# Top-k attention with a low-rank mixer and an MLP: where in a pair's fourth step the call stands that moves on a slab of parameters

## The chip, the cores and the metric

The kernel runs on one core of one Trainium2 chip, as one launch. The metric is the time of the whole launch on the device, in microseconds; the median of four runs before the change is 1765.66 us (1764.82 to 1766.17). The engines are named as the profile names them: PE is TensorE (matmuls; PEld its weight loads), DVE is VectorE, ACT is ScalarE, POOL is GpSimd, SP is SyncE, which here only issues DMAs. Each engine works through its own list of instructions in order and waits on semaphores for the others.

## What is computed

There are 8 batches, 8 heads, 576 positions and 64 values for each head. The first block is attention in which each row keeps only its 32 largest scores; its output, with the heads side by side (512 channels), goes into a low-rank mixer over the positions and an MLP over the channels (512 to 2048 to 512). The mixer's and the MLP's parameters come as 64-bit floats, q, k and v as 32-bit floats.

```
scores = (q @ k^T) / sqrt(64)
kth    = 32nd largest of each row
attn   = softmax(where(scores >= kth, scores, -1e9)) @ v
x      = attn with heads side by side               # (8, 576, 512)
u      = x + ((x^T @ U) @ V)^T                      # U: 576x32, V: 32x576
out    = u + max(u @ w_ch1, 0) @ w_ch2              # 512x2048, 2048x512
```

## The kernel before

**Steps.** The heads are taken in pairs, 4 pairs for each batch, 32 pairs in all. A pair has 5 steps: t = 0 to 3 take 128 rows of both heads (two score tiles of 128x576, called chunk 0 and chunk 1), and t = 4 takes the last 64 rows of both heads in one tile. Steps are numbered n = 5g + t through all pairs. One loop over n writes the instructions of all engines in an order set out by hand; no scheduler reorders them. The loop has three forms: one for the first batch's steps (n below 19, `ALONE` is 20), one for the two steps in which the first batch is finished (n = 19 and 20), and one for all later steps. In the later steps the MLP of the batch before is laid between the attention's work; in the first batch there is none yet.

**A step's selection.** For a score tile, VectorE finds the 8 largest values of each row (L385), and then in three rounds replaces those found by a very small number (L396) and finds the next 8 (L400). The last value of the third round is the 32nd largest. The generator `front` holds this: its first `next` gives L385, the next three the rounds 1 to 3. Behind round 3 the scores below the 32nd are pushed down. For chunk 1 GpSimd does it: a mask (L403) and an addition (L404). For chunk 0 it is done early in the following step: ScalarE makes the offset (L420) and the mask (L421), and GpSimd subtracts (L422). Then ScalarE takes the exponentials of both chunks (L351), in the middle of the following step. Three buffers for score tiles go round, so a new tile of scores is copied from PSUM (L344 to L346, on ScalarE) only where the exponentials of three steps before are done. In step 18 chunk 0 goes another way: ScalarE takes the exponential early, and VectorE multiplies it by the mask (L406) right behind round 3.

**Behind the exponentials.** TensorE transposes the weights (L475, L480), ScalarE copies them (L476, L481), TensorE multiplies with v (L509, L513, L499) and ScalarE copies the result (L522, L507). When a pair is through, `mixed` transposes back (L534, L538), divides by the sums on GpSimd (L539), and applies U and V (L545, L553, L557, L559, L567). After a batch's fourth pair the MLP's first products (L582, with ScalarE's L594) and second products (L601) follow.

**Parameters.** The 64-bit parameters come in 36 slabs, most of them 128x512 values. Each is turned to 32-bit floats by integer work on its words, in a line of three stages, and `next_params(1)` moves that line on by one slab. In this order a call

- issues what is left of the passes of the slab begun in the call before, on ScalarE: L174, L175, L178,
- joins that slab: a shift by 3 bits on VectorE (L186) and two integer additions on GpSimd (L187, L189),
- makes the slab loaded in the call before ready for its three passes; they are then issued one by one by the following calls of `fill` (or by the next call of `next_params`),
- issues the load of another slab on SP (L152).

So a slab is loaded in one call, passed over ScalarE after the next, and joined in the one after that. Three buffers hold the raw slabs. In the first batch's steps a call stands behind round 1 where t is 0 to 3, and a second one behind round 3 where t is 0 or 1; t = 4 has none. That makes 6 calls for a pair.

**fill.** Each `fill()` issues one waiting pass on ScalarE, moves `mixed` on by one stage, and, once there is an MLP to do, issues a share of it.

A step of the first batch is written in this order: what is left of chunk 0 of the step before (L420 to L422), the scores of the next step (on TensorE and ScalarE), the products with v of three steps before, transposes of two steps before, `fill`, round 1, a call of `next_params`, `fill`, round 2, the exponentials of the step before, `fill`, round 3, for t of 0 and 1 a second call, the mask and the addition for chunk 1 (L403, L404), `fill`.

Of the kernel before, what the change touches and what calls it, by code (L numbers as in the profile page):

```python
# [26 lines left out]
def kernel(  # L27
# [35 lines left out]
    NT, TAIL = 4, 64  # L63
# [221 lines left out]
    def prep(g):  # L285

        qkT = attn.tile([P, 2, S], F32, tag="qkT", name="qkT")
        qkTs[g] = qkT
        if blocked(g):
            nc.vector.transpose(qkT.rearrange("p i n -> p (i n)"), raw.pop(g))  # L290
            yield
            return
        tiles, ends = raw.pop(g)
        for i in (0, 2, 1) if g == 0 else (0, 1, 2):
            if i == 2:
                tp = ps_t.tile([P, 2, TAIL], F32, tag="tp", name="tp")
                nc.tensor.transpose(
                    tp.rearrange("p i n -> p (i n)"), ends.rearrange("p h d -> p (h d)"), ident
                )
                nc.scalar.copy(qkT[:, :, MAIN:S], tp)  # L300
                yield
                continue
            tp = ps_t.tile([P, NT, P], F32, tag="tp", name="tp")
            for c in range(NT):
                nc.tensor.transpose(tp[:, c, :], tiles[i][:, c].rearrange("p h d -> p (h d)"), ident)
            copy = nc.vector.tensor_copy if g == 0 and i else nc.scalar.copy
            copy(qkT[:, i, 0:MAIN], tp.rearrange("p t n -> p (t n)"))
            yield
# [54 lines left out]
    def eased(g, t):  # L363
        return bool(ways(g, t)[2])
# [70 lines left out]
    def shared(g, t):  # L435


        return t < NT and g * CH + t >= ROUNDED
# [22 lines left out]
    def turns(g, t):  # L461


        E2 = probs.pop((g, t))
        nh = 2 if t < NT else 1
        if shared(g, t):
            PT = PTs[g, t]
        else:
            PT = attn.tile([P, 2 * NT + 1, P], F32, tag="PT", name="PT")
            PTs[g, t] = PT  # L470
        for h in range(1 if shared(g, t) else nh):
            tp = ps_t.tile([P, NT, P], F32, tag="tp", name="tp")
            for j in range(NT):
                a = h * (S + TAIL) + j * P
                nc.tensor.transpose(tp[:, j, :], E2[:, a : a + P], ident)  # L475
            nc.scalar.copy(PT[:, NT * h : NT * h + NT], tp)  # L476
            yield
        tp = ps_t.tile([P, P], F32, tag="tp", name="tp")
        a = MAIN if nh == 2 else S - P
        nc.tensor.transpose(tp, E2[:, a : a + P], ident)  # L480
        nc.scalar.copy(PT[:, NT * nh], tp)  # L481
        yield

    def inverse(g, lo, hi):
        den = dens[g][:, lo:hi]
        if g == NPAIR - 1:
            nc.vector.tensor_scalar_add(den, den, 1e-9)
        nc.vector.reciprocal(den, den)

    def values(g, t):  # L490

        PT = PTs.pop((g, t))
        va, vd, vt = (a[g % NV] for a in (vas, vds, vts))
        O = ps_t.tile([P, P], F32, tag="tp", name="O")
        if t == NT:
            den, x = dens[g], xs[g % 2]
            inverse(g, 2 * NT if g == NPAIR - 1 else 0, 2 * NT + 1)
            for j in range(NT + 1):
                nc.tensor.matmul(  # L499
                    O,  # L500
                    lhsT=PT[:, j],
                    rhs=va[:, :, j, :] if j < NT else vt,
                    start=(j == 0),
                    stop=(j == NT),
                )
            for h in range(2):
                nc.scalar.mul(x[half(h), NT, half(h)], O[half(h), half(h)], den[half(h), 2 * NT :])  # L507
            return
        nc.tensor.matmul(O, lhsT=vd, rhs=PT[:, 2 * NT], start=True, stop=False)  # L509
        PB = PT[:, NT : 2 * NT].rearrange("p a (c j) -> p c a j", c=NT) if shared(g, t) else None  # L510
        for j in range(NT):
            for h in range(2):
                nc.tensor.matmul(  # L513
                    O[half(h)],
                    lhsT=va[:, h, j, :],
                    rhs=PB[:, j] if h and shared(g, t) else PT[:, NT * h + j],
                    start=False,
                    stop=(j == NT - 1),
                )
        if t == 0:  # L520
            XTs[g] = attn.tile([P, MAIN], F32, tag="XT", name="XT")
        nc.scalar.copy(XTs[g][:, cols(t)], O)  # L522
# [173 lines left out]
    t = 0  # L696
# [5 lines left out]
    for n in range(STEPS + 2):  # L702
        g, t = divmod(n, CH)
        if n < STEPS:
            if t == 0 and g + 1 < NP:
                load(g + 1)
            if t == 1 and g + 1 < NP:
                ready = prep(g + 1)
            fronts[n] = front(g, t)
            next(fronts[n])  # L710
        here, last = fronts.get(n, iter(())), fronts.pop(n - 1, iter(()))
        if n >= ALONE - 1 and n <= ALONE:

            if n < ALONE:
                next(last)
                values(*divmod(n - 3, CH))
                list(turning)
                next(here)
                next(last)
                scores(*divmod(n + 1, CH))  # L720
                values(*divmod(n - 2, CH))
            list(turns(*divmod(n - 1, CH)))
            values(*divmod(n - 1, CH))
            if n < ALONE:
                next(here)
                next(here)
                inverse(g, 0, 2 * NT)
                mixing.append(mixed(g, 1))
                fill()
                next(here)  # L730
                continue
            fill()
            scores(*divmod(n + 1, CH))
            next(here)
            while mixing:
                fill()
            next_params(1)
            fill()
            next(last, None)
            next(here)  # L740
            fill()
            next(here)
            next(here)
            fill()
            continue
        ease = eased(*divmod(n - 1, CH))
        if n < ALONE:
            if ease:
                next(last, None)
            scores(*divmod(n + 1, CH))  # L750
            if n >= 3:
                values(*divmod(n - 3, CH))
                if (n - 3) % CH == NT:
                    mixing.append(mixed((n - 3) // CH, 3))
            list(turning)
            fill()
            next(here)
            if t < NT:
                next_params(1)
            fill()  # L760
            next(ready, None)
            next(here)
            next(last, None)
            fill()
            next(here)
            if t in (0, 1):
                next_params(1)
            next(here)
            fill()
            if n >= 1:  # L770
                turning = turns(*divmod(n - 1, CH))
            continue
        away = n <= STEPS and shared(*divmod(n - 1, CH))
        if ease:
            next(last, None)
        fill()
        next(turning, None)
        fill()
        next(turning, None)
        if away:  # L780
            next(last)
        fill()
        next(turning, None)
        fill()
        if ease:
            next(last, None)
        if n - 2 >= ALONE:
            values(*divmod(n - 2, CH))
        if n + 1 < STEPS:
            scores(*divmod(n + 1, CH))  # L790
        next(here, None)
        next_params(1)
        if n - 2 >= ALONE and (n - 2) % CH == NT:
            mixing.append(mixed((n - 2) // CH, 5))
        fill()
        next(here, None)
        if away:
            blocks(*divmod(n - 1, CH))
        fill()
        if n <= STEPS:  # L800
            turning = turns(*divmod(n - 1, CH))
        fill()
        next(here, None)
        next(ready, None)
        if t in (1, 3):
            next_params(1)
        next(here, None)
        fill()
# [33 lines left out]
```

## Time and profile before

| what | value |
|---|---|
| median of 4 runs | 1765.66 us |
| profiled execution, its own time | 1766.04 us |
| its span, first to last instruction | 1764.3 us |
| PE busy | 1659.9 us (94%) |
| VectorE busy | 1540.1 us (87%) |
| ScalarE busy | 1027.4 us (58%) |
| GpSimd busy | 847.3 us (48%) |
| mean granted TensorE clock | 0.976 |
| DMA, mean | 64 GB/s |

The page cuts the span into 40 slices of 44 us; each digit is the busy share of an engine in tenths. Steps 0 to 18 of the first batch run from about 11 to 196 us, and the first product of an MLP starts at 212 us. The shares over the whole span are averages over these two stages. The timeline shows each instruction with its start, its duration, its line and operation, and in brackets how long the engine had been idle before and for whom. An instruction can be shown to start some 0.08 us before the one ahead of it on its engine ends. The chain of waits follows back from the last instruction, at each step to what released it.

### The profile page before, as it was taken

What the parts mean: (1) busy time and instruction counts of PE and PEld (TensorE: products, weight loads), DVE (VectorE), ACT (ScalarE), POOL (GpSimd) and SP (SyncE); (2) the same over time, 40 slices, a digit from 0 to 9 for tenths busy, and PEclk for the clock granted to TensorE, in tenths of its full rate; (3) what the DMA queues carried; (4) which work ended last, traced back from release to release, by engine and by line L of the source; (5) the groups of instructions that cost most, each with busy time, mean ns of one, the idle gap of its engine ahead of it and who ended that gap; (6) DMA issues with size and microseconds to landing.
All of it is one profiled execution on the core that took longest, in us unless ns stands there. A gap on an engine that the chain in (4) does not pass through costs nothing.

```text
span 1764.3 us, 28973 instructions
## 1 busy us (share of the span) xinstructions
PE 1659.9 (94%) x9851; PEld 1251.4 (71%) x9851; DVE 1540.1 (87%) x3106; ACT 1027.4 (58%) x2682; POOL 847.3 (48%) x591
## 2 busy tenths in 40 slices
PE   4565789999999999999999999999999999999999
PEld 2443556777777877788777877788777877788677
DVE  7999989999999999999999999999999999994000
ACT  4778777665655656565655566565656656564100
POOL 4777677444545454444444454545354554543000
PEclk7788899999999999999999999999999999999999
DMA  3232222233222222332322222323222232311010
GB/s 92 84 90 78 76 78 60 50 72 72 67 67 66 66 67 63 72 70 67 70 64 68 63 68 63 75 66 73 63 63 73 59 75 58 77 44 46 4 15 12
DMA packets 275828, 112.78 MB, mean 64 GB/s; under 512 B 173920, under 2 KB 260192, under 8 KB 275680
## 3 DMA queue, kind: packets, MB, share of 16 engines
q1 hardware_dynamic: 274624, 110.68, 26.0%
q8 instruction: 77, 1.26, 0.3%
q14 instruction: 71, 0.58, 0.1%
q10 hardware_dynamic: 1056, 0.26, 0.1%
HBM read 74.15 MB, written 36.70 MB: 63 GB/s over the span
## 4 chain that ended last, share of the span: by engine, by line
PE 77%; DVE 13%; POOL 4%; ACT 3%; issue 1%; DMA 1%; SPq 0%; POOLq 0%; DVEq 0%
PE mm L582 26%; PE mm L601 25%; PE sc L333 6%; PE O L513 6%; DVE rr L396 6%; DVE m L400 5%; PE tp L475 3%; DVE first L385 2%; PE sc L320 2%; PE O L499 2%; PE up L557 1%; PE O L509 1%; POOL E L403 1%; PE up L559 1%; PE tp L649 1%
## 5 line engine op out<-in xcount | busy, mean ns | idle before, releaser
L400 DVE MAX8 m<-rr 128x8 f32<-128x576 f32 x864 | 614.4, 748 | 5.5
L601 PE MATMUL mm<-hT,w 128*128 128x256 f32 (+1 forms) x2048 | 547.4, 410 | 0.0
L582 PE MATMUL mm<-uT,w 128*128 128x256 f32 (+1 forms) x2048 | 541.4, 410 | 2.7 <-ACT hT L594 2.7
L403 POOL TENSOR_SCALAR E<-Ssb,m 128x576 f32<-128x576 f32 x127 | 281.0, 2213 | 369.7 <-DVE m L400 362.9
L582 PEld LDWEIGHTS mm<-uT,w 128*128 128x128 f32 x2048 | 371.6, 190 | 116.3 <-issue 25.8
L601 PEld LDWEIGHTS mm<-hT,w 128*128 128x128 f32 x2048 | 368.3, 190 | 106.8 <-issue 22.5
L396 DVE MATCH_REPLACE8 rr<-m,rr 128x576 f32<-128x576 f32 x576 | 423.3, 741 | 0.0
L422 POOL TENSOR_TENSOR Ssb<-Ssb,E 128x576 f32<-128x576 f32 x159 | 225.3, 1417 | 141.0 <-ACT E L421 141.0
L594 ACT ACTIVATE hT<-mm 128x320 f32<-128x320 f32 (+1 forms) x256 | 105.2, 411 | 242.8 <-PE mm L582 242.5
L351 ACT ACTIVATE E<-Ssb,nmax 128x576 f32<-128x576 f32 x288 | 223.1, 776 | 39.8 <-POOL Ssb L404 30.3
L385 DVE MAX8 first<-Ssb 128x8 f32<-128x576 f32 x288 | 203.7, 744 | 37.5 <-ACT Ssb L346 36.7
L396 DVE MATCH_REPLACE8 rr<-first,Ssb 128x576 f32<-128x576 f32 x288 | 211.8, 742 | 0.0
L404 POOL TENSOR_TENSOR Ssb<-Ssb,E 128x576 f32<-128x576 f32 x127 | 179.3, 1411 | 10.6
L333 PE MATMUL sc<-qkT 64*128 64x288 f32 x1024 | 167.8, 448 | 8.9 <-ACT Ssb L344 7.8
L475 PE MATMUL tp<-ident,E 128*128 128x128 f32 x736 | 115.4, 282 | 38.3 <-ACT XT L522 15.9
L513 PE MATMUL O<-PT,va 128*64 128x128 f32 x2048 | 143.0, 281 | 1.6 <-DMA PT<-away 1.6
L475 PEld LDWEIGHTS tp<-ident,E 128*128 128x128 f32 x736 | 91.7, 145 | 69.4 <-ACT XT L522 17.8
L476 ACT COPY PT<-tp 128x512 f32<-128x512 f32 x184 | 106.8, 585 | 57.6 <-PE tp L475 56.3
L421 ACT ACTIVATE E<-Ssb,least 128x576 f32<-128x576 f32 x159 | 123.3, 775 | 5.2
L333 PEld LDWEIGHTS sc<-qkT 64*128 64x128 f32 x1024 | 91.8, 194 | 46.5 <-issue 14.2
L513 PEld LDWEIGHTS O<-PT,va 128*64 128x64 f32 x2048 | 111.6, 138 | 17.8 <-DMA PT<-away 2.1
L614 DVE TENSOR_TENSOR oT<-uT,mm 128x320 f32<-128x320 f32 (+1 forms) x8 | 3.6, 454 | 137.4 <-PE mm L601 137.4
(81 smaller groups left out, 1569.3 us busy)
## 6 DMA issues: line engine op xcount, KB each, us to landing
away<-y SPq DMA_DIRECT2D x416, 64.0 KB, 1.8
PT<-away SPq DMA_DIRECT2D x104, 256.0 KB, 2.6
raw<-in_moe_w_ch_dram SPq DMA_DIRECT2D x32, 512.0 KB, 3.8
va<-in_v_dram SPq DMA_DIRECT2D x64, 128.0 KB, 2.2
out_dram<-ob SPq DMA_DIRECT2D x57, 128.0 KB, 2.0
ld<-in_q_dram SPq DMA_DIRECT2D x108, 64.0 KB, 2.4
ld<-in_k_dram SPq DMA_DIRECT2D x108, 64.0 KB, 2.3
ld<-in_q_dram SPq DMA_DIRECT2D x108, 8.0 KB, 2.0
```

The lines of the kernel that those rows point to most:

```text
L333: nc.tensor.matmul(sc[:, h, 0:HALF], lhsT=qkT[half(h), 0, cols(t)], rhs=qkT[half(h), 1, i * HALF : (i + 1) * HALF], start=True, stop=True,)
L351: nc.scalar.activation(E, chunk, AF.Exp, bias=nmax, scale=SCALE, accum_out=total)
L385: nc.vector.max(ms[c], curs[c])
L396: nc.vector.match_replace(nxt, ms[c], curs[c], NEG)
L400: nc.vector.max(ms[c], curs[c])
L403: nc.gpsimd.tensor_scalar(Es[c], chunks[c], ms[c][:, 7:8], NEG, ALU.is_lt, ALU.mult)
L404: nc.gpsimd.tensor_tensor(chunks[c], chunks[c], Es[c], ALU.add)
L422: nc.gpsimd.tensor_tensor(chunks[c], chunks[c], Es[c], ALU.subtract)
L475: nc.tensor.transpose(tp[:, j, :], E2[:, a : a + P], ident)
L513: nc.tensor.matmul(O[half(h)], lhsT=va[:, h, j, :], rhs=PB[:, j] if h and shared(g, t) else PT[:, NT * h + j], start=False, stop=(j == NT ...
L582: nc.tensor.matmul(ph[:, 0:w], lhsT=w1[:, cc, f * P : (f + 1) * P], rhs=uT[:, cc, lo:hi], start=(cc == 0), stop=(cc == NC - 1),)
L601: nc.tensor.matmul(po[:, 0:w], lhsT=w2[:, f, c * P : (c + 1) * P], rhs=hTs[f][:, 0:w], start=(f == 0), stop=(f == NF - 1),)
```

## The change

Two conditions change in the first batch's form of a step. Where t is 3, the call of `next_params` behind round 1 falls away, and a call behind round 3 is made, between round 3 and the mask and addition for chunk 1. That concerns steps 3, 8, 13 and 18. The number of calls and the order of the slabs stay as they were. The order of instructions stays the same on TensorE and on SP; it changes on VectorE (the shift L186), on GpSimd (L187 and L189, which come out in the same row but now wait for a later shift) and on ScalarE (the three passes).

```
             list(turning)
             fill()
             next(here)
-            if t < NT:
+            if t < NT - 1:
                 next_params(1)
             fill()
             next(ready, None)
             next(here)
             next(last, None)
             fill()
             next(here)
-            if t in (0, 1):
+            if t in (0, 1, NT - 1):
                 next_params(1)
             next(here)
             fill()
```

More of the change, by code (lines that the diff above doesn't have):

```diff
@@ L757 @@
             next(here)
-            if t < NT:
+            if t < NT - 1:
                 next_params(1)
@@ L765 @@
             next(here)
-            if t in (0, 1):
+            if t in (0, 1, NT - 1):
                 next_params(1)
```

## The prediction

> **What bounds the kernel now.** I name a step by n = 5g + t (pair g, step t); the four moved calls stand in steps 3, 8, 13 and 18. First I read the page's table of slices: up to slice 5 (about 220 us) VectorE is full and TensorE is not; afterwards TensorE is full.
>
> ```profile
> PE   4565789999999999999999999999999999999999
> ...
> DVE  7999989999999999999999999999999999994000
> ```
>
> Busy time by window then says how full: after the length come the busy us (and instructions) of PE, PEld, DVE, ACT and POOL, then clock and DMA.
>
> ```profile
> 53.00:101.00 48.00, 30.89 (x196) 20.61 (x196) 47.69 (x100) 38.93 (x93) 38.17 (x27) 0.79 0.28 82
> ```
>
> VectorE has 47.69 of 48.00 us, ScalarE 38.9, GpSimd 38.2. VectorE's waits between 36 and 258 us are an empty list. So in the first batch a microsecond saved on VectorE counts, and a wait elsewhere counts only if it reaches VectorE. Next I looked at the moved call's own VectorE instruction, the shift at L186, in VectorE's timeline (start, us, what):
>
> ```profile
> 45.47 1.38 DVE L186 TENSOR_SCALAR w<-w 128x512 uint32<-128x512 uint32 x1
> ...
> 93.20 1.40 DVE L186 TENSOR_SCALAR w<-w 128x512 uint32<-128x512 uint32 x1
> ...
> 109.85 0.41 DVE L186 TENSOR_SCALAR w<-w 128x512 uint32<-128x512 uint32 x1
> ...
> 140.94 1.41 DVE L186 TENSOR_SCALAR w<-w 128x512 uint32<-128x512 uint32 x1
> ...
> 188.71 1.40 DVE L186 TENSOR_SCALAR w<-w 128x512 uint32<-128x512 uint32 x1
> ```
>
> Exactly the four moved ones (45, 93, 141, 189) take 1.4 us; alone, as at 109.85, it takes 0.41. GpSimd's timeline shows why:
>
> ```profile
> 92.91 1.41 POOL L404 TENSOR_TENSOR Ssb<-Ssb,E 128x576 f32<-128x576 f32 x1
> 94.27 1.59 POOL L422 TENSOR_TENSOR Ssb<-Ssb,E 128x576 f32<-128x576 f32 x1
> ...
> 99.67 2.21 POOL L403 TENSOR_SCALAR E<-Ssb,m 128x576 f32<-128x576 f32 x1 [1.18 <-DVE m L400]
> 101.97 1.41 POOL L404 TENSOR_TENSOR Ssb<-Ssb,E 128x576 f32<-128x576 f32 x1
> 103.33 1.41 POOL L422 TENSOR_TENSOR Ssb<-Ssb,E 128x576 f32<-128x576 f32 x1
> 106.96 1.41 POOL L422 TENSOR_TENSOR Ssb<-Ssb,E 128x576 f32<-128x576 f32 x1 [2.21 <-ACT E L421]
> ```
>
> The shift of 93.20 falls in L404 (92.91 to 94.32), ends 0.28 after it, and the next L422 is stretched to 1.59. A shift beside GpSimd's L403 is not held (72.41, 0.41 us, within L403's 71.15 to 73.38). So shift and two-operand adds exclude each other. The chain of waits prices it on the path: 1.32 us against 0.33.
>
> ```profile
> 93.28 1.32 DVE w L186
> ...
> 109.93 0.33 DVE w L186
> ```
>
> **The change, part by part.** Each call moves one shift on VectorE, two adds on GpSimd (L187, L189), three passes on ScalarE (L174, L175, L178) and one load on SP, from behind round 1 to behind round 3.
>
> 1. *The shift leaves its place.* The next round starts at 93.20 instead of 94.52: 1.32 us (1.30, 1.33, 1.32 in the other three).
>
> 2. *The shift in its new place*, right behind round 3 (step 8: 100.08 - 1.32 = 98.76). GpSimd's L422 of the step before ends by 95.9, and nothing can be on GpSimd, since L187 waits for this very shift. Price 0.33, as at 109.93. Net 0.97, 0.99, 1.00 us in steps 3, 8, 13. In step 18 the instruction behind round 3 is L406, at 195.81 where round 3 ends at 195.59: a 0.22 us gap the shift fills. So 1.21 there.
>
> 3. *The adds now stand ahead of L403.* In step 8: shift 98.76, L187 0.48 later (as 109.85 to 110.33) at 99.24, L403 2.63 after that (as 164.02 to 166.65) at 101.87, L404 +2.30 at 104.17, L422 +1.36 at 105.53. That is 2.2 us later than the 103.33 of before. Behind them wait the exponentials L351 on ScalarE, then L420, L421 and transposes of that tile. Cover: the score tile that VectorE needs for step 10 is copied before these exponentials, and step 11's copies finish near 109.9 against a need at 115.1 (116.06 - 0.99). Without that cover, 2.2 us per call would be lost.
>
> 4. *A new meeting.* L351 (second half) 0.04 behind that add's end at 106.94 is 106.98, L420 0.77 later, L421 +0.23, L422 of step 9 +0.85: 108.83. The shift of step 10 now comes at 109.85 - 0.99 = 108.86. Before, the two were 2.9 us apart. Likewise 61.10 against 61.13, and 156.58 against 156.59. If GpSimd is first, the next round starts 0.20 after its add ends (94.32 to 94.52 shows that): 108.83 + 1.41 + 0.20 = 110.44 against 110.17, so 0.27 slower than now (0.30 and 0.27 in the other two) instead of 0.99 faster. These are the bounds for the three: -2.96 or +0.84. Who asks first? GpSimd's adds take 0.26, 0.46 and 1.29 us for 32, 128 and 512 columns, so about 0.18 is fixed. A held shift ends 0.28 after the add while its own work is 0.33, so GpSimd lets go some 0.05 before its end, and about 0.13 of its fixed part lies ahead of its data: it would ask near 108.96. VectorE's shift stands behind a maximum that ends 0.08 after the shift's shown start, so it asks by 108.94. I take VectorE first, narrowly: -2.96.
>
> 5. *ScalarE's passes* (0.55 + 0.66 + 0.65 on the chain) go from step t = 3 into the next. In step 9 they end near 104.1, before L404 releases the exponentials at 105.6: nothing. At the last pair they matter: L175 and L178 no longer stand before L420 at 196.34, but L175 falls before L538 (205.64) and L178 behind L507.
>
> L420 could run near 195.0, but L422 of step 18 stands behind L189: L187 194.75, L189 196.12, L422 197.40 (197.31 before). Its exponential starts at 198.84, the score copy L344 at 199.60 instead of 200.46, and L538 0.78 earlier with L175 before it. L178 delays L187 of step 20 to about 208.9 (208.08 before); its cover is L403 of step 20, which waited 2.34 us for VectorE. Nothing.
>
> 6. *Handing over.* GpSimd's L539 would end near 206.56 and the shift of step 20 start at 206.39: it is held, 0.05 us lost. So VectorE carries 1.16 of the 1.21.
>
> 7. *The load on SP.* The order of SP's queue is unchanged and each slab is used two calls later; price 0, at worst 3.8 us once, its median landing time.
>
> [...] L406 reads two tiles from SBUF, and no row of before shows one beside a GpSimd add. [...]
>
> **Sum.** Steps 3, 8, 13: 0.97 + 0.99 + 1.00 = 2.96; step 18: 1.16; together 4.1 us. It reaches the end because VectorE drives GpSimd's chain at 225.7 (L187 0.13 behind the shift that ends at 225.58), whose exponentials release ScalarE and the score copy at 258.43; behind that the order is fixed. The profiled execution took 1766.04 (span 1764.3 and 1.7 around it), 0.38 over the median 1765.66. So 1761.9 for that execution and 1761.6 against the median.
>
> **The rivals.** The measurement tells about 0.2%, 3.5 us, from no change.
> - *GpSimd has the ports first wherever the two meet* (slower). For it: its shown starts are 0.01 to 0.03 earlier. Price +0.84, and L406 held by L187 to 196.05 makes step 18 +0.24: +1.1, 1766.8. With the phases changed, the shifts between 207 and 302 us may be held too, 1.0 each: seven are free there now (207.60, 225.20, 229.60, 246.84, 280.23, 284.63, 294.80). From three of them it is over 0.2% slower: 1769.8. It decides at three meets 0.03 us wide. Against: point 4.
> - *Some meets each way*: one lost costs 1.2 of the 4.1: 1762.8 to 1764.
> - *VectorE's lead is not passed on.* The chain between 164 and 212 us runs over GpSimd and ScalarE, which are full there. Then only ScalarE's 0.78 remains: 1764.9. Against: that chain starts from a shift of VectorE (163.48, step 15), so it moves with it, and GpSimd idles 3.26 us just before.
>
> **How the numbers follow.** The sum's case has 0.55; three quarters of it is beyond 0.2% (the sum lies 0.6 over that bound, and a part may be lost at the handover): 0.41 faster. GpSimd first 0.20, of which 0.15 has held shifts later and is slower by over 0.2%. Mixed 0.10, not passed on 0.15. Within 0.2%: 0.14 + 0.05 + 0.10 + 0.15 = 0.44. Range: 1761.0 (4.2 us at most from the four, and 0.4 of the 2.0 that held shifts at 217, 240 and 272 could give) to 1766.9 (GpSimd first, without later ones).
>
> **What would show it.** Four shifts of 0.41 us right behind round 3 in steps 3, 8, 13, 18; L403 there 2.2 us later; the first maximum of step 19 near 192.4 (196.55 before) if the meets go to VectorE, near 196.2 if to GpSimd; three shifts of steps 5, 10, 15 at 0.41 or at 1.6; L538 near 201.9. A VectorE wait on the score copy before 250 us would prove me wrong about the cover, and so would a first expansion product (L582, 212.28 before) no earlier than before.

## The result and the profile after

| | median | executions | lowest to highest |
|---|---|---|---|
| before | 1765.51 us | 57 | 1764.44 to 1766.96 |
| changed | 1762.50 us | 37 | 1759.48 to 1763.93 |

The ratio is 0.9982, with a 95% interval of 0.9977 to 0.9986: 0.18% faster, 3.0 us by the medians. It lies inside the predicted range (1761.0 to 1766.9), 0.9 us above the predicted 1761.6, and just within the 0.2% up to which I had counted a result as no change; the interval leaves no change out. The profiled execution took 1761.78 us (span 1760.0), 4.3 us less than that of before; it is one of the faster ones, so it is not typical of the median, and that difference turns out to be the interesting part.

The page's table of slices of the changed kernel looks as before: VectorE is full at the start, TensorE afterwards.

```profile
PE   4566889999999999999999999999999999999999
...
DVE  7999988999999999999999999999999999994000
```

The same window as before, busy us (and instructions) of PE, PEld, DVE, ACT and POOL, then clock and DMA:

```profile
53.00:101.00 48.00, 30.56 (x197) 20.48 (x198) 47.59 (x101) 39.37 (x96) 39.26 (x28) 0.79 0.28 82
```

VectorE is still the full engine, with 47.59 of 48.00 us. GpSimd has risen from 38.17 to 39.26 us: part of that is one more instruction in the window, part is adds that now wait inside their own time. VectorE's timeline shows the four moved shifts (L186), three that they now bring near GpSimd's adds, and the masked product L406 behind the last of them:

```profile
51.15 0.40 DVE L186 TENSOR_SCALAR w<-w 128x512 uint32<-128x512 uint32 x1
...
61.25 0.41 DVE L186 TENSOR_SCALAR w<-w 128x512 uint32<-128x512 uint32 x1
...
97.88 0.41 DVE L186 TENSOR_SCALAR w<-w 128x512 uint32<-128x512 uint32 x1
...
107.99 0.41 DVE L186 TENSOR_SCALAR w<-w 128x512 uint32<-128x512 uint32 x1
...
144.63 0.40 DVE L186 TENSOR_SCALAR w<-w 128x512 uint32<-128x512 uint32 x1
...
154.74 0.41 DVE L186 TENSOR_SCALAR w<-w 128x512 uint32<-128x512 uint32 x1
...
191.38 0.40 DVE L186 TENSOR_SCALAR w<-w 128x512 uint32<-128x512 uint32 x1
191.71 0.80 DVE L406 SCALAR_TENSOR_TENSOR E<-Ssb,m,E 128x576 f32<-128x576 f32 x1
```

All four that took 1.4 us take 0.40 or 0.41. In the three narrow meetings (61, 108, 155) VectorE's shift went first (0.41 us each) and GpSimd's add waited. GpSimd's timeline beside it:

```profile
98.37 1.29 POOL L187 TENSOR_TENSOR w<-w,raw 128x512 uint32<-128x512 uint32 x1 [3.53 <-DVE w L186]
99.74 1.28 POOL L189 TENSOR_TENSOR w<-w,raw 128x512 uint32<-128x512 uint32 x1
101.00 2.21 POOL L403 TENSOR_SCALAR E<-Ssb,m 128x576 f32<-128x576 f32 x1
103.29 1.41 POOL L404 TENSOR_TENSOR Ssb<-Ssb,E 128x576 f32<-128x576 f32 x1
...
107.94 1.73 POOL L422 TENSOR_TENSOR Ssb<-Ssb,E 128x576 f32<-128x576 f32 x1 [1.88 <-ACT E L421]
...
191.86 1.82 POOL L187 TENSOR_TENSOR w<-w,raw 128x512 uint32<-128x512 uint32 x1 [3.53 <-DVE w L186]
193.76 1.29 POOL L189 TENSOR_TENSOR w<-w,raw 128x512 uint32<-128x512 uint32 x1
195.00 1.41 POOL L422 TENSOR_TENSOR Ssb<-Ssb,E 128x576 f32<-128x576 f32 x1
```

L422 is shown to start at 107.94, 0.05 before the shift of 107.99, and is the one that waits: 1.73 instead of 1.41. In steps 5 and 15 the two starts are 0.04 and 0.03 apart and the adds take 1.72 and 1.71. At 191.86 L187 takes 1.82 instead of 1.29, beside L406, which reads two tiles from SBUF. The chain of waits now prices the moved shift like a free one:

```profile
97.97 0.32 DVE w L186
...
108.07 0.33 DVE w L186
```

I follow VectorE's lead by the start of the first maximum (L385) of a step, in the changed kernel minus before (worked out from the timelines; at step 3 it is +0.13, an offset from ahead of the change):

| step | before | changed | difference |
|---|---|---|---|
| 4 | 52.33 | 51.47 | -0.86 |
| 9 | 100.08 | 98.21 | -1.87 |
| 14 | 147.83 | 144.96 | -2.87 |
| 19 | 196.55 | 192.44 | -4.11 |
| 22 | 225.50 | 220.93 | -4.57 |
| 25 | 258.43 | 253.12 | -5.31 |
| 32 | 334.20 | 328.89 | -5.31 |
| end of the span | 1764.3 | 1760.0 | -4.3 |

So the four steps give 0.99, 1.01, 1.00 and 1.24 us. Behind step 19 the lead wanders. The 0.46 between steps 19 and 22 come from VectorE's shift of step 21, which took 0.86 us beside an L422 in before (217.57) and takes 0.41 in the changed kernel (213.46). By step 25 another 0.74 is gained, and 1.0 is lost behind 334 us. Which of that is the change and which is chance the experiments had to show.

### The profile page after: what moved, and what is told of

Its sections match the earlier page's. It is cut to its first block, busy times and chain, and to the rows that moved or that the text cites. A ratio compares the mean times of both kernels' runs of the same rounds, so it can differ in the third digit from the quotient of the medians.

```text
span 1760.0 us, 28970 instructions
## 1 busy us (share of the span) xinstructions
PE 1664.2 (95%) x9851; PEld 1255.3 (71%) x9851; DVE 1535.9 (87%) x3106; ACT 1027.7 (58%) x2682; POOL 848.2 (48%) x591
## 4 chain that ended last, share of the span: by engine, by line
PE 76%; DVE 16%; POOL 3%; ACT 2%; issue 2%; SPq 1%; DMA 1%; POOLq 0%; DVEq 0%
PE mm L582 26%; PE mm L601 25%; DVE rr L396 7%; PE sc L333 7%; DVE m L400 6%; PE O L513 6%; PE tp L475 3%; DVE first L385 2%; PE sc L320 2%; PE O L499 2%; PE up L557 1%; PE O L509 1%; PE tp L649 1%; PE up L559 1%; PE tp L534 1%
## 5 line engine op out<-in xcount | busy, mean ns | idle before, releaser
L403 POOL TENSOR_SCALAR E<-Ssb,m 128x576 f32<-128x576 f32 x127 | 281.2, 2214 | 361.8 <-DVE m L400 344.7
L422 POOL TENSOR_TENSOR Ssb<-Ssb,E 128x576 f32<-128x576 f32 x159 | 225.7, 1419 | 138.0 <-ACT E L421 138.0
L594 ACT ACTIVATE hT<-mm 128x320 f32<-128x320 f32 (+1 forms) x256 | 105.3, 411 | 243.5 <-PE mm L582 242.9
L351 ACT ACTIVATE E<-Ssb,nmax 128x576 f32<-128x576 f32 x288 | 223.0, 776 | 38.1 <-POOL Ssb L404 27.2
L385 DVE MAX8 first<-Ssb 128x8 f32<-128x576 f32 x288 | 203.8, 744 | 36.9 <-ACT Ssb L346 36.1
L404 POOL TENSOR_TENSOR Ssb<-Ssb,E 128x576 f32<-128x576 f32 x127 | 179.3, 1412 | 10.6
L333 PE MATMUL sc<-qkT 64*128 64x288 f32 x1024 | 169.6, 453 | 8.7 <-ACT Ssb L344 7.8
L513 PE MATMUL O<-PT,va 128*64 128x128 f32 x2048 | 145.7, 284 | 1.3 <-DMA PT<-away 1.3
L513 PEld LDWEIGHTS O<-PT,va 128*64 128x64 f32 x2048 | 113.8, 140 | 17.8 <-DMA PT<-away 1.6
L333 PEld LDWEIGHTS sc<-qkT 64*128 64x128 f32 x1024 | 92.9, 197 | 46.4 <-issue 14.2
```

Source lines behind the costliest of these rows:

```text
L333: nc.tensor.matmul(sc[:, h, 0:HALF], lhsT=qkT[half(h), 0, cols(t)], rhs=qkT[half(h), 1, i * HALF : (i + 1) * HALF], start=True, stop=True,)
L351: nc.scalar.activation(E, chunk, AF.Exp, bias=nmax, scale=SCALE, accum_out=total)
L385: nc.vector.max(ms[c], curs[c])
L403: nc.gpsimd.tensor_scalar(Es[c], chunks[c], ms[c][:, 7:8], NEG, ALU.is_lt, ALU.mult)
L404: nc.gpsimd.tensor_tensor(chunks[c], chunks[c], Es[c], ALU.add)
L422: nc.gpsimd.tensor_tensor(chunks[c], chunks[c], Es[c], ALU.subtract)
```

## The experiments

The theory at the start was that of the prediction: exclusion of shift and adds, four places. Differences are to the runs of before on the same chip. With nine to eleven executions of each variant the interval of a ratio is about 0.0009 to each side, 1.6 us, so differences between two variants that are smaller than this are read from rows and not from times.

### The same again

No edit: the changed kernel a second time.

> The changed kernel once more, for a second profile and the spread of its times. Theory (the moved shift no longer waits for GpSimd's adds, and in steps 5, 10 and 15 the shift and GpSimd's L422 start almost together): a profile in which all three shifts of steps 5, 10, 15 take 0.41 us goes with a time 4 us below before; each of them shown at 1.6 us goes with 1.2 us less gain, which would make the spread of 1759.5 to 1763.9 us. Rival (the spread has another source): all three at 0.41 us and a time above 1763.

Measured: 1762.77 us (1762.03 to 1763.50) against 1765.25, ratio 0.9984 (0.9975 to 0.9992). The profiled execution took 1763.5, and it is not the same as the first one. GpSimd's division L539 and the shift of step 20 on VectorE, first in the changed kernel's first profile, then in this one:

```profile
203.49 0.41 DVE L186 TENSOR_SCALAR w<-w 128x512 uint32<-128x512 uint32 x1
...
203.68 1.11 POOL L539 TENSOR_TENSOR x<-x,den 128x512 f32<-128x512 f32 x1 [7.26 <-ACT x L538]
```

```profile
202.94 1.04 POOL L539 TENSOR_TENSOR x<-x,den 128x512 f32<-128x512 f32 x1 [6.79 <-ACT x L538]
...
203.25 1.02 DVE L186 TENSOR_SCALAR w<-w 128x512 uint32<-128x512 uint32 x1
...
213.84 1.02 DVE L186 TENSOR_SCALAR w<-w 128x512 uint32<-128x512 uint32 x1
```

In the first, the shift comes 0.19 ahead of L539 and is free. In the second, L539 is 0.31 ahead, and the shift takes 1.02; the shift of step 21 is held too. VectorE's lead falls from 4.35 at step 19 to 3.57 at step 22, where the first profile had 4.57. This is the meeting that the prediction's step 6 had priced at 0.05 us. The three narrow meetings went to VectorE here as in the first profile (0.41 each), and the time is above 1763: by the expectation's own terms they do not make the spread.

### The narrow meetings of steps 5, 10 and 15

One run takes them away, the other gives them to GpSimd. In the first the call of those steps moves behind round 2:

```
-            if t < NT - 1:
+            if t < NT - 1 and (t > 0 or n == 0):
                 next_params(1)
...
             next(here)
+            if t == 0 and n > 0:
+                next_params(1)
             next(last, None)
```

> As the changed kernel, but in steps 5, 10 and 15 the first call stands behind round 2 and not behind round 1, so that its shift comes 2.8 us after the place where L422 of the short step starts. Theory: the shifts of steps 3, 8, 13, 18 stay at 0.41 us, no L422 of steps 4, 9, 14 is stretched, the time is 4 us below before (1761.5) and its spread shrinks to that of before, about 2.5 us. Rival (the near-coincidence is not the cause of the spread): the same median as the changed kernel, 1762.5, and the same spread of over 4 us.

Measured: 1762.83 us (1761.27 to 1764.26), ratio 0.9985 (0.9976 to 0.9994), the same as the changed kernel beside it (1762.77). The adds L422 are no longer stretched; the shift of step 20 takes 1.15, behind an L539 that starts 0.18 ahead of it. So the narrow meetings cost nothing as they fall, and they are not what spreads the executions. I had thought that they might be; that theory falls.

The second run puts a small maximum of 0.21 us ahead of the call in steps 5, 10 and 15 (a tile of 128x8 is added for its result; line numbers behind it are one higher):

```
+            if t == 0 and n > 0:
+                nc.vector.max(idle, ident[:, 0:64])
             if t < NT - 1:
                 next_params(1)
```

> As the changed kernel, with one small VectorE instruction (a maximum over 64 columns of the identity, about 0.2 us, its result unused) ahead of the first call of steps 5, 10 and 15, so that the shift asks 0.2 us later than L422. Theory: now GpSimd always has the ports first, each of the three shifts takes about 1.4 us instead of 0.41, and with the small instruction itself each pair loses 1.2 to 1.4 us: 3.6 to 4.2 us more than where VectorE is first, 1765.3 to 1765.9. Rival (the order of two starts does not matter): 0.2 us for each pair, 0.6 in all, 1763.1.

Measured: 1766.10 us (1764.90 to 1767.16), ratio 1.0002 (0.9993 to 1.0011), 3.3 us more than the changed kernel measured beside it. The meeting of step 5 in its timeline, VectorE and GpSimd:

```profile
61.26 0.21 DVE L760 MAX8 idle<-ident 128x8 f32<-128x64 f32 x1
61.38 1.50 DVE L187 TENSOR_SCALAR w<-w 128x512 uint32<-128x512 uint32 x1
...
61.20 1.40 POOL L423 TENSOR_TENSOR Ssb<-Ssb,E 128x576 f32<-128x576 f32 x1 [1.88 <-ACT E L422]
```

The shift is shown 0.18 behind the add instead of 0.04, and now it is the one that waits; the two other meetings go the same way (1.54 and 1.53). The first maximum of step 19 starts at 196.20, 3.76 later than the 192.44 of the changed kernel. Some 0.1 us in the order of two engines decides the whole gain. The prediction's first rival, GpSimd first in all three (its "has the ports" says no more than that; what the two engines share, no run shows), forecast 1766.8 for this order; the run, which carries 0.6 us of added maxima besides, took 1766.10.

### Which part carries the gain

Step 18 alone:

```
-            if t < NT - 1:
+            if t < NT and n != ALONE - 2:
                 next_params(1)
...
-            if t in (0, 1, NT - 1):
+            if t in (0, 1) or n == ALONE - 2:
                 next_params(1)
```

> The change in step 18 alone; steps 3, 8 and 13 as before. Theory: 1.2 us for VectorE at step 19, of which the meet with L539 in step 20 takes back 0.5 to 0.7: 0.4 to 1.2 us in the end, 1764.1 to 1764.9. Rival (the last pair's call carries most of the gain, by ScalarE's passes leaving the path to the first MLP product): 2.5 us or more, 1762.8 or less.

Measured: 1766.23 us (1764.79 to 1767.32) against 1765.88, ratio 1.0000 (0.9991 to 1.0009), above the expected 1764.1 to 1764.9. The 1.21 us are there on VectorE: the first maximum of step 19 starts at 195.34 instead of 196.55. Two steps later half of them are gone. VectorE and GpSimd in this run:

```profile
206.39 1.04 DVE L186 TENSOR_SCALAR w<-w 128x512 uint32<-128x512 uint32 x1
...
206.11 1.04 POOL L539 TENSOR_TENSOR x<-x,den 128x512 f32<-128x512 f32 x1 [6.80 <-ACT x L538]
...
217.01 1.03 DVE L186 TENSOR_SCALAR w<-w 128x512 uint32<-128x512 uint32 x1
```

L539 is 0.28 ahead, the shift of step 20 waits, and the lead is 0.57 at step 21 (212.91 against 213.48) and 0.39 at step 22 (225.11 against 225.50). In before the same shift stood at 207.60, behind the end of L539 (206.30 and 1.04 long): VectorE's own gain moved the shift into the division.

Steps 3, 8 and 13 without step 18:

```
-            if t < NT - 1:
+            if t < NT - 1 or n == ALONE - 2:
                 next_params(1)
...
-            if t in (0, 1, NT - 1):
+            if t in (0, 1) or (t == NT - 1 and n != ALONE - 2):
                 next_params(1)
```

> The change in steps 3, 8 and 13 alone; step 18 as before. Theory: 0.97 + 0.99 + 1.00 = 3.0 us, and step 20's shift and L539 keep the distance that they have before, so nothing is given back: 1762.3, with a spread like that of before (2.5 us), the same median as the whole change. Rival (the last pair's call carries most): under 1.5 us, 1763.8 or more.

Measured: 1763.29 us (1762.01 to 1764.30) against 1765.88, ratio 0.9986 (0.9977 to 0.9995): 2.6 us, where 3.0 were expected. The lead is 2.80 at step 19, the shift of step 20 is free (204.80, 0.41), and at step 22 the lead is still 2.81. By the medians the three steps give nearly all of the 3.0 us.

The third run leaves the calls where they were before and takes out what the shifts met: the additions L404 and L422 of the tiles of steps 2, 7, 12 and 17.

```
-            nc.gpsimd.tensor_tensor(chunks[c], chunks[c], Es[c], ALU.add)
+            if t != 2 or g >= NPAIR:
+                nc.gpsimd.tensor_tensor(chunks[c], chunks[c], Es[c], ALU.add)
...
-            nc.gpsimd.tensor_tensor(chunks[c], chunks[c], Es[c], ALU.subtract)
+            if t != 2 or g >= NPAIR:
+                nc.gpsimd.tensor_tensor(chunks[c], chunks[c], Es[c], ALU.subtract)
```

> The kernel before with the calls where they were, but GpSimd's L404 and L422 left out for the tiles of steps 2, 7, 12 and 17 (their scores below the 32nd are then not pushed down, so part of the selection is left out). Theory (only those additions hold the shift of the following step): the shifts of steps 3, 8, 13 and 18 take 0.41 us in their old place and the time falls by 4.0 us, to 1761.4, with nothing moved. Rival (the shift's 1.4 us has another cause, such as ScalarE's pass or the place behind round 1): 1.4 us as before and a gain under 1 us.

Measured: 1763.15 us (1761.79 to 1764.15) against 1765.88, ratio 0.9982 (0.9973 to 0.9991). The four shifts in their old place, at 45.67, 92.42, 139.19 and 185.93, take 0.40 each. The lead is 3.78 at step 19; the shift of step 20 is held (203.83, 1.15), and 2.85 is left behind it. Without the adds, nothing of the change is needed to get its gain: VectorE's lead grows by 0.97 to 1.00 us at each of the four steps, the price of one held shift.

### The handing over at step 20

First another place for the moved call, behind round 2 of t = 3:

```
             next(here)
+            if t == NT - 1:
+                next_params(1)
             next(last, None)
             fill()
             next(here)
-            if t in (0, 1, NT - 1):
+            if t in (0, 1):
                 next_params(1)
```

> Neither the old place nor the new one: in steps 3, 8, 13 and 18 the call stands behind round 2. Theory (what counts is only that the shift does not fall in an add of GpSimd): L422 of the step before ends at 95.7 and the shift would come at 96.0, so all four shifts take 0.41 us; the adds are through before L403, which is not delayed, and nothing meets the shift in step 10: 3.0 us for the first three pairs and about 1.0 for the last, 1761.5. Rival (the gain comes from ScalarE's passes leaving the last pair's path, or from the place at the step's end as such): under 1.5 us of gain, 1764 or more.

Measured: 1762.14 us (1760.50 to 1762.55) against 1765.25, ratio 0.9976 (0.9967 to 0.9985). The four shifts (48.39, 95.14, 141.90, 188.89) take 0.40 to 0.41; the lead is 3.59 at step 19, less than in the changed kernel, but the shift of step 20 is free (204.01, 0.41), and at step 22 the lead is 4.05.

Then the changed kernel with the call of step 20 one round later, out of the way of L539:

```
-            next_params(1)
             fill()
             next(last, None)
             next(here)
+            next_params(1)
             fill()
```

> As the changed kernel, but in step 20 the call stands behind round 2 and not behind round 1. Theory (the spread and the lost microsecond come from step 20, where the shift meets GpSimd's addition-like L539: 0.41 us in one profile, 1.02 and 1.15 in two others): the shift of step 20 comes 2.8 us later, when L539 is through, and takes 0.41 us; L385 of step 22 stays 4.5 us ahead of before; 1761.3 us, and no run above 1762.6. Rival (the spread is from the clock or from elsewhere in the later stretch): 1762.5 to 1762.8 with runs up to 1763.9, as for the changed kernel.

Measured: 1761.71 us (1760.39 to 1762.56) against 1765.88, ratio 0.9975 (0.9965 to 0.9984), 4.2 us below before. It is the lowest median of all, though the ratio of the place behind round 2, 0.9976, can't be told from it. GpSimd's division and the moved shift:

```profile
203.25 1.05 POOL L539 TENSOR_TENSOR x<-x,den 128x512 f32<-128x512 f32 x1 [6.80 <-ACT x L538]
...
206.32 0.41 DVE L186 TENSOR_SCALAR w<-w 128x512 uint32<-128x512 uint32 x1
```

The lead is 4.05 at step 19 and 4.51 at step 22, with L539 as early as it likes. This is what the prediction's 4.1 us look like where they are handed on. That it beats the changed kernel is not shown by the times: the intervals overlap (0.9965 to 0.9984; 0.9977 to 0.9986 for the changed kernel and 0.9975 to 0.9992 for its repetition). The rows show that it keeps at step 20 what the repetition lost there (4.51 against 3.57 at step 22); the first profile of the changed kernel had kept it too (4.57).

I call it the best version below. Its nine executions lie in two groups, four at 1760.4 to 1760.6 and five at 1761.7 to 1762.6, and its profiled one, of the upper group, loses 1.7 us of lead between 350 and 360 us.

### The clock behind 350 us

At that place TensorE idles twice, for PT from ScalarE and then for a DMA. TensorE's timeline of the changed kernel:

```profile
349.31 1.03 PE L582 MATMUL mm<-uT,w 128*128 128x256 f32 x4
351.14 0.49 PE L509 MATMUL O<-PT,vd 128*128 128x128 f32 x2 [0.81 <-ACT PT L481]
351.56 0.43 PE L513 MATMUL O<-PT,va 128*64 128x128 f32 x2
353.33 1.18 PE L513 MATMUL O<-PT,va 128*64 128x128 f32 x14 [1.33 <-DMA PT<-away]
354.44 2.29 PE L333 MATMUL sc<-qkT 64*128 64x288 f32 x8
```

The same place in before, 5.3 us later:

```profile
356.46 0.49 PE L509 MATMUL O<-PT,vd 128*128 128x128 f32 x2 [0.76 <-ACT PT L481]
...
358.94 1.09 PE L513 MATMUL O<-PT,va 128*64 128x128 f32 x14 [1.63 <-DMA PT<-away]
359.96 1.24 PE L333 MATMUL sc<-qkT 64*128 64x288 f32 x8
```

Eight products L333 take 2.29 us after and 1.24 before. The windows that follow these waits, columns as above, say why; first the changed kernel, then before:

```profile
354.00:358.00 4.00, 4.00 (x18) 2.52 (x15) 2.21 (x5) 2.46 (x7) 0.00 (x0) 0.57 0.31 70
```

```profile
358.00:362.00 4.00, 3.06 (x26) 2.33 (x27) 2.93 (x5) 3.36 (x10) 1.30 (x1) 1.00 0.15 40
```

The granted clock is 0.57 in the one and 1.00 in the other. Comparing the leads ahead of and behind such a stretch, it costs 0.8 to 1.0 us in the changed kernel, in its repetition, with step 18 alone and with the call behind round 2, 1.2 and 1.3 with steps 3, 8 and 13 and without the adds, and 1.7 in the best version; the run without the narrow meetings has the same two waits (0.81 and 1.41), a clock of 1.00 behind them, and no loss. Theory: the idle time brings the half clock; fill it, and the upper group goes. Twelve products of the MLP are drawn ahead (the first attempt on the best version and on before; two more on the best version):

```
         if ease:
             next(last, None)
+        if n - 2 == ROUNDED:
+            for _ in range(12):
+                due -= next(fillers[0], 0.0)
         if n - 2 >= ALONE:
             values(*divmod(n - 2, CH))
```

> The changed kernel with the call of step 20 behind round 2 and, in the step whose gap at 351 to 353 us leaves TensorE idle for 0.8 and 1.3 to 1.6 us, twelve products of the MLP drawn from the filler ahead of the values of the tile, so that TensorE has work in that gap. Theory (the half granted clock at 354 to 359 us follows the idle time just ahead of it): no stretch under 0.8 of clock between 350 and 362 us, the lead of VectorE over before at the end stays at 5.0 to 5.4 us instead of falling to 3.8, and the time is 1760.0 to 1760.9. Rival (the dip has another cause, such as its own period): a dip there as in the kernel without the products, and a time of 1761.7. A third outcome: the twelve products moved ahead are missed later as filler, the dip is gone and the time is 1761.5 to 1763.

> The kernel before with the same twelve products drawn ahead into the gap at 351 to 353 us and nothing else. The profiled execution of before shows no dip there, so by the theory (the dip follows the idle time, in some executions) the products take away only what the other executions lose: 0 to 0.9 us, a time of 1764.7 to 1765.7, at its likeliest 1765.0, with no execution above 1766.2. Rival (the dip has another cause): the same as before, 1765.5, with the same spread. If the twelve products are missed later: 1766 to 1767.

Measured: 1763.04 us (1762.22 to 1764.83) and 1768.36 us (1767.45 to 1769.76), against 1766.23; ratios 0.9985 (0.9976 to 0.9994) and 1.0012 (1.0004 to 1.0021). Both missed: I had placed the products two steps of the loop too early. On the best version they ran at 333 us, where TensorE had work anyway, and were then lacking: the wait ahead of L509 grew from 0.81 to 1.95 us on the best version (no dip behind it) and to 1.95 on before (a dip to 0.54 at 358 us). The times lie at or above the upper end of the outcome in which the products are missed later.

The second attempt writes `ROUNDED + 2`, once with the twelve subtracted from what the next calls of `fill` issue, once without (`next(fillers[0], 0.0)` in place of the subtraction).

> The changed kernel with the call of step 20 behind round 2 and twelve products of the MLP drawn ahead directly in front of the values whose first product waited 0.81 us for PT at 351 us (one step of the loop later than two steps above in the first attempt, where they came at 332 us and enlarged the idle time). Twelve at 0.23 us take 2.75 us, more than the 0.81 and 1.44 us that TensorE idles there. The twelve are subtracted from the shares of the next fillers. Theory (the half clock at 354 to 359 us follows that idle time): TensorE's idle time between 350 and 356 us is 0.5 us or less, no stretch under 0.8 of clock between 350 and 362 us, and the time is 1760.0 to 1760.9. Rival (the dip comes by another cause): a dip there all the same, 1761.0 to 1762.5. Third outcome: the idle time only moves to a later gap that the twelve had filled, with or without a dip there, 1761.5 to 1763.

> The same twelve products at the same place, but not subtracted from the shares of the next fillers, so the MLP's products run twelve ahead from there on. Theory: as for the kernel with the subtraction, 1760.0 to 1760.9, and the later gaps are filled as before. If the fillers were missed in the other one, this one is faster than it by up to 2 us. Against it: VectorE and GpSimd get their tiles up to 2.75 us later behind 355 us, which costs up to that where TensorE does not have the last word: up to 1763.

Measured: 1765.80 us (1764.82 to 1767.60) and 1765.88 us (1764.56 to 1767.02) against 1766.50, ratios 0.9999 (0.9990 to 1.0008) and 0.9996 (0.9988 to 1.0005). Both missed again. TensorE's timeline of the one with the subtraction:

```profile
353.68 4.15 PE L582 MATMUL mm<-uT,w 128*128 128x256 f32 x18 [2.20 <-ACT hT L594]
...
362.75 0.61 PE L509 MATMUL O<-PT,vd 128*128 128x128 f32 x2 [1.80 <-ACT PT L481]
363.29 1.98 PE L513 MATMUL O<-PT,va 128*64 128x128 f32 x16
```

The products can't fill the gap: they wait for ScalarE's L594 themselves, 2.20 us, and push the values L509 from 351.03 (in the best version) to 357.67. So the gap was not there for lack of issued work, and this way of filling it is closed. For the clock, the runs still say something. Behind the idle time of 2.20 us, which ends at 353.68 in the one and at 354.61 in the other, neither kernel shows a dip; behind the 1.80 us at 361 to 363 the first one does (0.74, 0.50 and 0.90 in the 2-us windows from 362). The size of the idle time alone doesn't decide.

What the traces do show is a grid. In all 14 profiles every stretch at one granted clock, between the first change and the last, lasts a whole number of 3.41 us; behind 200 us each dip lasts 3.41 us, that of the best version 6.83. Where it lies against the program differs from execution to execution: counted from the span's start, its remainder is 2.62 us in the changed kernel, 2.38 in before and 1.16 in the repetition. Cut at it, the window that holds most of the idle time and the one behind it, first in the changed kernel, then in before:

```profile
350.78:354.19 3.41, 1.71 (x18) 1.33 (x18) 3.12 (x6) 1.62 (x6) 3.13 (x3) 1.00 0.24 77
354.19:357.60 3.41, 3.41 (x14) 2.02 (x11) 1.62 (x5) 2.29 (x7) 0.00 (x0) 0.50 0.29 65
```

```profile
357.37:360.78 3.41, 1.84 (x20) 1.53 (x22) 3.23 (x6) 2.17 (x7) 1.93 (x2) 1.00 0.31 98
360.78:364.19 3.41, 3.41 (x18) 2.72 (x15) 2.45 (x7) 2.58 (x7) 0.10 (x1) 1.00 0.27 60
```

TensorE was busy for 1.71 of 3.41 us in the window ahead of the dip, and for 1.84 where none followed (2.00 in the run without the narrow meetings). Over all 14 profiles, behind 200 us, half clock followed each of the 16 windows at full clock in which TensorE was busy for less than 0.43 of the time, 7 of the 24 between 0.43 and 0.61, and none above. That fits nearly the same waits bringing a dip or not by where the grid cuts them; no run shows it alone. Between 0.43 and 0.61 the busy share as shown does not decide: the second attempt without the subtraction had 0.43 ahead of 354 us and no dip.

## Why the prediction was right in its direction and off in its size

1. *The shift leaves its place.* Right: the price of a held shift, 1.32 against 0.33 on the chain, and its cause. Taking out the adds gave the same gain without moving anything.
2. *The new place.* Right: predicted net 0.97, 0.99, 1.00 and 1.21, measured 0.99, 1.01, 1.00 and 1.24 us. Four shifts of 0.40 to 0.41.
3. *Adds ahead of L403.* Right: predicted 101.87 without the earlier gain of step 3, measured 101.00 with it; L403 of step 3 is 2.35 us later than before (54.27 against 51.92). The cover held: VectorE's only waits between 36 and 258 us come to 4.2 us, of which 3.98 are the one before the maximum of 253.12, where before waited 5.26 at the same instruction (it starts at 258.43 there, just behind the window of the prediction's empty list).
4. *The new meetings.* Right, and as narrow as told. All three went to VectorE in both profiles of the changed kernel; some 0.1 us later they go to GpSimd and the time is 1766.1. My reason (some 0.13 us of GpSimd's fixed part ahead of its data) fits what the runs show: shown 0.03 to 0.05 ahead GpSimd loses, shown 0.15 to 0.18 ahead it wins. Right behind another of its adds it wins even when shown 0.06 ahead (235.31 against 235.37 in the changed kernel, where the shift took 1.63) and 0.10 ahead (239.67 against 239.77 in before, 1.59). Where the tie lies for a GpSimd that idled before, as in the three meetings, was not measured. The rival's +0.24 for an L406 held by L187 is shown by no run: L406 of step 18 took 0.80 to 0.82 us in all 14 profiles, 0.81 in the one that gave the three meetings to GpSimd, and where an L187 is shown beside it, L187 took longer (1.82 and 1.80 instead of 1.29).
5. *ScalarE's passes.* The direction was right, the size not. The score copy L344 of the last pair starts at 197.70 (196.96 in the repetition), where the step, with the lead of 2.96, gives 196.64. L422 ahead of it starts at 195.00 (194.74) instead of 194.44. Why is said below the list.
6. *Handing over.* This is the step that failed: "it is held, 0.05 us lost". In the repetition L539 started at 202.94 and not at 202.56 (205.52 in the step's phase, less 2.96), the shift at 203.25 and not at 203.43 (that profile runs 0.15 ahead from the start), so the shift waited 0.6 us; at step 21's shift, held for 1.02 us where before had 0.86, another 0.16 of the lead went. The 1.16 us that I let step 18 carry to the end were, alone, worth 0.39 on VectorE at step 22 and nothing clear of noise in the time (ratio 1.0000), and some 0.4 beside the other three (3.0 against 2.6 us by the medians, less than the intervals can tell).
7. *The load.* Nothing to see of it, as predicted.

Two things lie between step 6 and the rows; both made GpSimd's L539 later than the step has it. The first is a meeting for which step 5 has no term: L187 with L406 of step 18. In before GpSimd idles beside L406 (195.81; its L422 follows at 197.31). Beside L406 L187 took 1.82 us in the changed kernel and 1.80 in the repetition, instead of 1.29. With it L422 ended at 196.41, and at 196.15 in the repetition, where the step has 195.86 (197.40 + 1.42 - 2.96). In the repetition the exponential L351 that waits for it started at 196.19, right behind it. In the first profile it started at 196.94, 0.53 us later, because ScalarE was not free sooner; there the longer L187 cost nothing.

The second is TensorE's granted clock, which the step does not have at all. Up to 200 us it changes between 0.50 and 1.00, and a stretch at 0.50 ended at 186.7 us in before, at 186.9 in the first profile and at 185.5 in the repetition. There TensorE makes the 16 products and 8 transposes that ScalarE's chain to these exponentials begins with. L513 in before, in the first profile and in the repetition:

```profile
187.10 1.09 PE L513 MATMUL O<-PT,va 128*64 128x128 f32 x16
```

```profile
184.53 1.98 PE L513 MATMUL O<-PT,va 128*64 128x128 f32 x16
```

```profile
184.29 1.66 PE L513 MATMUL O<-PT,va 128*64 128x128 f32 x16
```

In before the full clock was back for them; in the changed kernel they came 2.6 and 2.8 us earlier, still at half clock. So the chain's lead over before fell from 2.88 (first profile) and 3.11 us (repetition) at L509 just ahead to 1.47 and 2.25 at L480 behind (189.46, 187.99, 187.21). ScalarE won part of it back without its two passes, to 2.76 and 3.50 at L344, where the step has 3.82. In the repetition L422 and ScalarE's own work ended within 0.04 us of each other, so either alone would have made L539 that late, and no run takes them apart. In the first profile the clock alone did it, and by 0.7 us more (L538 at 203.02 against 202.30 in the repetition, 0.27 of it an offset from the start), so that L539 missed the shift and the lead was handed on, by luck. The sum was 4.1 us, and 3.0 was measured. Not every GpSimd instruction holds a shift: in the first batch six shifts of before within an L403 took 0.40 or 0.41.

Behind the first batch the clock comes in again. The profiled execution of before ran 3.4 us at half clock at 238 us and had no dip at 358; the changed one's dips lie at 259 and 354. Between 247 and 258 us the lead over before grew by 0.9 us in nine of the 13 other profiles, those without a dip at 233 to 241 us, and not at all in the four that have one there. That is why the table of leads shows 5.31 at step 25, more than the change can give, and 4.3 at the end. The agreement of that execution's 4.3 with the predicted 4.1 is therefore partly luck; the median's 3.0 is the number to explain, and by the medians it is 2.6 from steps 3, 8 and 13 and next to nothing from step 18.

The chances followed the same step: with a sum of 3.5, the 4.1 less the 0.6 us for which the repetition's shift of step 20 waited, the likeliest case would have stood on the bound of 0.2%, where the result lies.

## What to carry to other kernels

Where two engines exclude each other, a held instruction is shown by its own length (1.40 against 0.41 us here), and moving it by one round is worth the difference; but every later meeting of the same two engines shifts with the gain, so write down the phase of each one up to the end of the stage, above all those by which the gain is handed on. A meeting that is 0.05 us wide is a tie, and its price stands with its full size in the range. The term that a gain is passed on needs the same care as the gain: of 1.2 us won in step 18, 0.6 were lost at step 20 and 0.8 by step 22. And a chain that runs through TensorE moves against the grid of its clock: the same products took 1.09 or 1.98 us here.

## What was not expected of the hardware

- The engine with the later shown start can go first: in the meetings of steps 5, 10 and 15 VectorE's shift, shown 0.03 to 0.05 us behind GpSimd's add, took 0.41 while the add took 1.71 to 1.73; shown 0.15 to 0.18 behind, it took 1.50 to 1.54.
- The half granted clock behind about 2 us of idle TensorE comes in some executions and not in others, with the same work and nearly the same gaps: 0.76 and 1.63 us without (before), 0.81 and 1.33 with (changed), 0.81 and 1.41 without (no narrow meetings), 0.81 and 1.44 with (best version), 2.20 without (both second attempts). It costs 0.8 to 1.7 us, as much as the change's fourth step. The grid of 3.41 us, its phase changing from execution to execution, is what these traces show. The window ahead of the dip was not idle: TensorE was busy for 0.50 to 0.52 of it in the changed kernel, its repetition and the best version. What exactly is counted in a window stays open.
- The two groups of executions of the best version, 1.7 us apart, fit a dip present or absent, but each kernel has only one profiled execution; that was argued, not shown.
